# Gate sums on TensorE, one more MLP bank and a new head order in a gated attention and mixer kernel

## The chip, the cores and the metric

The kernel runs on one core of a Trainium2 chip. The metric is the time of one execution in microseconds (us), as the device gives it, and the median of the runs counts. The engines are named as the profile names them: PE is TensorE's matmul, PEld its weight load, DVE is VectorE, ACT is ScalarE, POOL is GpSimd, and SP is the queue that issues the DMAs.

## What is computed

The reference works on 4 batches of 768 tokens with 8 heads of 48 values, which makes 384 columns. Three layers follow each other.

```python
f = 1.0 / (1.0 + np.exp(-f_logit))
for t in range(S):                                  # gated linear attention, S = 768
    state = f[:, :, t, :, None] * state + einsum('bhd,bhe->bhde', k[:, :, t], v[:, :, t])
    y[:, :, t] = einsum('bhd,bhde->bhe', q[:, :, t], state)
xn = (x - mu) / np.sqrt(var + 1e-06) * g_ln         # x is y, heads side by side
x = x + np.maximum(xn @ w_ch1, 0.0) @ w_ch2         # first MLP, 384 -> 1536 -> 384
h = np.maximum(x.transpose(0, 2, 1) @ w_tok1, 0.0) @ w_tok2
u = x + h.transpose(0, 2, 1)                        # token mixing, 768 -> 256 -> 768
out = u + np.maximum(u @ w_ch1b, 0.0) @ w_ch2b      # second MLP
```

## The kernel before

The attention is cut into 24 units: unit n is chunk n // 4 (128 tokens) of batch n % 4. Within a unit the recurrence is turned into matrix products. The logarithms of the gates are summed along the 128 tokens, `ek` and `eq` are the exponentials of plus and minus these sums, K is multiplied by `ek` and Q by `eq`, and then masked products of K, Q and V and a carried state give `y`. The steps of a unit have short names, and the prediction uses them with the number of the unit in front, as in 3.y: `lf`, `lq`, `lv` load gates, K and Q, and V; `clamp` bounds the gate logits from below on DVE; `log` is an Exp and an Ln on ACT; `scan` is the running sum along the tokens on DVE (`tensor_tensor_scan`); `ek`, `eq` and `tot` are exponentials on ACT; `km` and `qm` are the two products; `kp` transposes K on PE and `kt` copies it out; `sc` and `st` are the score and state products on PE; `A0` and `A1` mask the scores on DVE; `stm`, `ste` and `std` carry the state on; `y` and `z` are the two halves of the output on PE, and `yw` is a one-element write between them, for which `z` waits; `lna`, `lnc` and `lnv` are the layer norm; `tp` transposes its result on PE, and `ah` and `al` split that into a high and a low part for the MLP.

The first MLP takes three units at a time, so it has 8 steps; steps 0 and 1 run as a pair. `m0.5` is block 5 (of 12) of the first product of step 0: nine matmuls of 384 columns in a PSUM bank. `m0.h5` on ACT and `m0.l5` on DVE (line L556) read this bank and write the hidden values' high and low parts `hh` and `hl`. `m0.o10` is a piece of the second product. The weights come as 64-bit numbers: `w5.ld` loads a block, `w5.a`, `.b` and `.c` turn it into fp32 on DVE (L201, L206, L211), `w5.h` rounds the high part on ACT and `w5.l` gives the rest, on DVE or POOL. `s` jobs do the same for the later layers' weights and store them in DRAM.

Each engine works through its instructions in the order in which they are recorded. Up to slot 77 (the head and the pair of steps 0 and 1) that order is the hand-written table `ORDER`; behind it each step has a slot number of its own, and the numbers are sorted. A `+45` behind an entry of the table puts 45 filler matmuls on zeros in front of this step's PE work: `busy` writes 224 columns, and `outp`, for `y`, writes three times as many matmuls of 64 columns. `WARM0` puts 56 fillers at the very start of PE.

PSUM has 8 banks: three in the pool `mmp` (first MLP blocks, second-product sums and `tp`), one in `atp` (`kp` alone) and four for the scores (`sc`). A bank of `mmp` goes round in turn, so a block waits until the block three places before it has been read by both ACT and DVE.

Token mixing and the second MLP (the `rt`, `ht`, L883 and L936 groups) begin behind step 7. The range check at the end decides on a flag whether a slow general path must be run; it isn't run with these inputs.

Of the kernel before, what the change touches and what calls it, by code (L numbers as in the profile page):

```python
# [29 lines left out]
JT = DTOK // 128  # L30
EPS = 1e-6
# [20 lines left out]
    1.ek 0.lq w14.ld 0.qm 1.lq w14.a 4.lf 2.scan 1.eq 0.km w12.ld 0.kp+45 4.clamp 1.qm 1.tot 2.ek 0.sc 4.log w2.ld
    w14.b 1.km 4.scan 3.ek 0.lv 0.tot 2.eq 0.kt w2.a 3.eq w12.a w2.b w12.b w14.c 3.tot 2.lq w14.h w2.c 1.kp+29
    1.sc 0.st 0.A0 0.A1 2.km 1.lv 5.lf 0.y+11 0.stm 1.kt w12.c 1.st 2.qm 0.yw 0.z 3.lq 0.ste 1.A1 0.lna 2.lv w14.l
    w4.ld 1.A0 1.stm 2.kp 5.clamp 1.y+3 w3.ld 0.lnc 1.ste 2.sc+8 5.log w1.ld 1.yw 2.kt 0.tp 3.km 5.scan 2.st 1.z
    2.A0 2.A1 3.kp 2.y+3 w2.h w12.h 2.stm 1.lna w2.l 3.qm 4.lq w12.l 1.lnc 2.ste 2.yw w1.a w3.a w4.a 3.lv 4.lv
    5.eq 4.ek 4.eq w1.b w3.b 5.ek w4.b 4.km w3.c w1.c 2.tot 0.ah w4.c 3.kt 3.sc+11 4.qm 0.lnv 1.tp 2.z 5.tot 2.lna
    w1.h 3.st w4.h 1.ah 3.A1 3.A0 4.kp 6.lf 2.lnc w3.h 4.kt 3.y+24 w0.ld 2.tp 4.sc 2.ah 1.lnv 4.st 3.stm 1.al
    4.tot 3.yw w5.ld 3.z 0.al 2.al 6.clamp w17.ld 4.A0 w1.l 4.A1 2.lnv w13.ld w5.a w3.l w4.l 3.lna 5.lq w0.a 6.log
    w5.b w16.ld 6.lv 0.std w0.b 3.ste m0.1 w5.c w5.h w5.l w0.c 6.scan 4.y m0.2 m0.h1 4.yw 4.stm 5.qm w0.h m0.h2  # L60
    m0.l1 m0.3 w0.l w22.ld m0.l2 4.z 3.lnc m0.h3 m0.4 m0.l3 w17.a w13.a 4.lna 5.km 6.lq 5.lv m0.0 7.lf 5.kp m0.h4
    6.eq 6.ek m0.h0 w15.ld w13.b w17.b w13.c m0.5 m0.l4 4.ste 5.sc 5.kt w13.h 4.lnc m0.h5 5.st w17.c 6.km m0.l0
    5.A1 3.tp 6.kp 4.tp 5.A0 3.ah 3.lnv m0.l5 6.qm 5.y w13.l w15.a w16.a 1.std 7.lv 7.clamp 6.sc w15.b w7.ld
    m0.o10 6.kt 4.ah 6.st 3.al 4.al w17.h w15.c 6.tot m0.o20 m0.o00 5.yw w16.b w17.l w16.c 6.A0 w15.h 5.stm w16.h
    w16.l w9.ld 5.z w15.l 2.lnr m0.o11 5.lna 7.log 6.A1 5.lnc m0.o21 w7.a w10.ld m0.r11 7.scan 5.tp 5.ah w7.b 5.al
    6.y 2.std w6.ld 7.lq 8.lf w7.c m0.r21 m0.o01 5.ste 6.yw m0.r01 7.tot 7.ek 7.eq m1.2 m1.0 w11.ld 6.stm w9.a
    m1.1 w10.a 4.lnv 7.km w10.b 8.clamp m1.h0 w9.b w7.h w9.c 6.z m1.h2 w18.ld m1.h1 8.lq m1.l0 m1.l2 w9.h w10.c
    m1.3 w9.l w6.a 7.kp w7.l m1.4 w22.a w6.b 8.log 7.qm m1.h3 m1.l1 m1.h4 w22.b m1.l3 7.sc w6.c w22.c w10.h w8.ld
    6.lna m1.5 w22.h 7.kt w22.l m1.h5 8.scan m1.l5 w11.a s1.ld m1.l4 w11.b 8.eq 6.lnc m1.o10 w6.h 7.st 4.std 10.lf
    m1.o20 8.tot 8.ek 5.lnv w11.c w10.l w8.a 5.lnr 9.lf w20.ld 6.ste 7.A0 7.A1 m1.o11 w11.h m1.o21 9.clamp 5.std  # L70
    9.log w8.b m1.o00 m1.r11 7.y m0.7 m1.r21 w8.c 3.std m1.o01 m0.h7 w6.l w20.a 9.scan m0.l7 7.yw 7.stm 8.km
    m1.r01 6.std w11.l m1.10 m1.9 m0.6 w8.h m1.h9 m0.h6 9.eq w19.ld w8.l 7.z 10.clamp m1.l9 8.qm 9.tot 10.log
    w18.a w19.a m1.7 w18.b 9.lq m0.l6 m1.h7 m1.h10 w20.b m1.l7 8.sc m1.l10 m1.8 w18.c m0.10 m1.h8 m0.8 m0.h10
    w18.h 9.ek w21.ld w20.c m1.l8 10.scan w19.b w18.l 9.km m0.h8 7.ste 8.kp w23.ld 9.lv m0.l8 8.lv w20.h 7.lna
    m1.6 11.lf 8.kt m0.9 10.lv 9.qm m1.h6 10.tot 8.st m0.h9 w20.l w19.c s0.ld m1.l6 w23.a w21.a 9.kp 10.eq 7.std
    9.kt m0.11 w23.b w19.h m0.h11 m0.l9 m0.l10 8.A0 6.tp 8.A1 w21.b m1.11 m0.l11 8.y m1.h11 w19.l 10.ek 6.ah 7.lnc
    w23.c 8.stm 8.yw w21.c m1.o12 8.z 9.sc s1.a w21.h 6.al w23.h s1.b w21.l m0.o22 m1.l11 8.ste 7.tp 11.clamp
    11.log w23.l 10.lq s0.a 9.st 7.lnv 8.lna m0.o23 9.A1 11.scan 11.ek 11.eq 9.stm 9.A0 m0.r23 9.ste m1.o13 9.y
    8.lnc m1.r13 6.lnv 10.km 7.ah 9.yw s1.c 10.qm m0.o02 8.tp 8.ah 8.al 10.kp 8.lnv 10.sc 7.al 9.z m0.o12 m0.o03
    10.kt 10.st s0.b m0.o13 10.stm m1.o02 10.A0 m0.r13 m0.r03 m1.o22 m1.d1 s3.ld m1.o03 9.std 9.lna 8.std 10.ste  # L80
    s0.c 10.A1 10.std s2.ld m0.d0 s0.h m0.d2 m1.o23 9.lnc m1.r03 11.lq 11.lv m1.d0 8.lnr m0.d1
""".split()

# [211 lines left out]

# [1045 lines left out]
```

## Time and profile before

| What | us |
|---|---|
| median of 3 runs (779.31 to 783.74) | 781.45 |
| the profiled execution | 782.92 |
| span of its trace, first to last instruction | 781.2 |
| PE busy in the span | 756.5 |

The span is what the trace shows, and the execution's own time is 1.7 us more. The execution that was profiled is 1.5 us above the median. The page gives busy time by engine and the chain that ended last; a window gives the busy time of each engine in one stretch; PEclk is the clock that TensorE was granted, where 1.00 is 2.4 GHz and 0.50 is 1.2 GHz.

### The profile page before, as it was taken

How to read it: one execution, taken by the hardware profiler on the slowest of the kernel's cores; microseconds unless marked ns; L12 is line 12 of the kernel's file. 1: busy time of each engine (PE TensorE's matmuls, PEld its weight loads, DVE VectorE, ACT ScalarE, POOL GpSimd, SP SyncE). 2: the span in 40 equal slices, each digit the busy share in tenths (PEclk: the TensorE clock that was granted, in tenths of full speed). 3: DMA queues.
4: the chain of work that ended last, by engine and by line, in shares of the span. 5: the costliest groups of instructions: out<-in, count | busy, mean ns of one | idle time of the engine just before them, and what ended most of it. 6: DMA issues, size and time to landing. Idle time of an engine off the chain costs nothing.

```text
span 781.2 us, 17469 instructions
## 1 busy us (share of the span) xinstructions
PE 756.5 (97%) x7129; PEld 735.0 (94%) x7129; DVE 516.9 (66%) x950; ACT 355.2 (45%) x851; POOL 152.9 (20%) x125
## 2 busy tenths in 40 slices
PE   8899999999999999999999999999999999999996
PEld 7689999989899898999999999999999999999996
DVE  7588877577787657765343664786558673878481
ACT  6454545244544444443131442564337442666440
POOL 1243333234444223330000010100001010101010
PEclk9999999999999999999999999999999999999999
DMA  8565442457647465553255985335343544343401
GB/s 249 152 217 178 149 142 77 150 166 230 216 147 230 137 183 189 168 186 123 74 161 212 344 305 177 93 113 160 110 143 102 161 126 134 99 144 101 137 21 66
DMA packets 61433, 122.54 MB, mean 157 GB/s; under 512 B 6944, under 2 KB 26784, under 8 KB 60576
## 3 DMA queue, kind: packets, MB, share of 16 engines
q1 hardware_dynamic: 61344, 121.33, 48.8%
q8 instruction: 58, 0.95, 0.5%
q14 instruction: 31, 0.25, 0.1%
HBM read 96.93 MB, written 24.38 MB: 155 GB/s over the span
## 4 chain that ended last, share of the span: by engine, by line
PE 86%; DVE 4%; DMA 3%; issue 2%; ACT 2%; POOL 1%; SPq 1%; POOLq 0%; DVEq 0%
PE mo L936 19%; PE mo L567 18%; PE mm L883 16%; PE mm L537 15%; PE rt L803 3%; PE ht L825 3%; PE sc L394 2%; PE sc L403 2%; DMA ts<-t_d 1%; PE sc L340 1%; PE sc L352 1%; PE tp L501 1%; PE kp L317 1%; PE tp L837 1%; DMA F<-in_f_t 1%
## 5 line engine op out<-in xcount | busy, mean ns | idle before, releaser
L537 PE MATMUL mm<-wx 128*128 128x384 f32 x864 | 161.5, 339 | 4.9 <-DVE hl L556 4.9
L537 PEld LDWEIGHTS mm<-wx 128*128 128x128 f32 x864 | 148.6, 188 | 8.0 <-DVE hl L556 7.5
L883 PE MATMUL mm<-xsh,wx 128*128 128x384 f32 x528 | 138.1, 335 | 0.9 <-DVE q L899 0.9
L567 PE MATMUL mo<-w2h,hh 128*128 128x384 f32 x288 | 99.0, 344 | 1.0 <-DVE hl L556 0.8
L883 PEld LDWEIGHTS mm<-xsh,wx 128*128 128x128 f32 x528 | 95.8, 188 | 1.5 <-PE mm L883 1.2
L936 PE MATMUL mo<-w2h,hh 128*128 128x384 f32 x288 | 97.0, 337 | 0.0
L567 PE MATMUL mo<-w2h,hl 128*128 128x384 f32 x288 | 96.4, 335 | 0.0
L567 PE MATMUL mo<-w2l,hh 128*128 128x384 f32 x288 | 96.3, 334 | 0.0
L936 PE MATMUL mo<-w2h,hl 128*128 128x384 f32 x288 | 96.3, 334 | 0.0
L936 PE MATMUL mo<-w2l,hh 128*128 128x384 f32 x288 | 96.2, 334 | 0.0
L923 POOL TENSOR_TENSOR hl<-u,hh 128x768 fp32r<-128x768 f32 x16 | 29.7, 1853 | 339.9 <-ACT u L918 246.0
L883 PE MATMUL mm<-xsl,wx 128*128 128x384 f32 x264 | 88.2, 334 | 0.0
L552 ACT ACTIVATE hh<-mm 128x384 fp32r<-128x384 f32 x96 | 46.3, 486 | 64.8 <-PE mm L537 60.1
L556 DVE SCALAR_TENSOR_TENSOR hl<-mm,hh 128x384 fp32r<-128x384 f32 x96 | 52.7, 551 | 27.5 <-ACT hh L552 27.2
L940 DVE TENSOR_TENSOR xr<-mo,xr 128x384 f32<-128x384 f32 x48 | 26.7, 556 | 54.2 <-PE mo L936 54.2
L1094 ACT ACTIVATE cs<-cs 128x384 f32<-128x384 f32 x56 | 31.1, 555 | 59.3 <-DVE cs L1091 59.1
L567 PEld LDWEIGHTS mo<-w2h,hh 128*128 128x128 f32 x288 | 54.1, 188 | 2.0 <-DVE hl L556 1.1
L936 PEld LDWEIGHTS mo<-w2h,hh 128*128 128x128 f32 x288 | 54.1, 188 | 0.1
L567 PEld LDWEIGHTS mo<-w2l,hh 128*128 128x128 f32 x288 | 54.1, 188 | 0.0
L936 PEld LDWEIGHTS mo<-w2l,hh 128*128 128x128 f32 x288 | 54.1, 188 | 0.0
L567 PEld LDWEIGHTS mo<-w2h,hl 128*128 128x128 f32 x288 | 54.1, 188 | 0.0
L936 PEld LDWEIGHTS mo<-w2h,hl 128*128 128x128 f32 x288 | 54.1, 188 | 0.0
(163 smaller groups left out, 1359.5 us busy)
## 6 DMA issues: line engine op xcount, KB each, us to landing
cs<-in_w SPq DMA_DIRECT2D x48, 384.0 KB, 3.1
sg<-in_w SPq DMA_DIRECT2D x44, 384.0 KB, 4.4
ts<-t_d SPq DMA_DIRECT2D x48, 256.0 KB, 3.0
wx<-f_d SPq DMA_DIRECT2D x6, 1152.0 KB, 11.4
V<-in_v_n SPq DMA_DIRECT2D x21, 288.0 KB, 4.7
F<-in_f_t SPq DMA_DIRECT2D x21, 224.0 KB, 3.6
T<-in_k_t SPq DMA_DIRECT2D x21, 224.0 KB, 2.7
T<-in_q_t SPq DMA_DIRECT2D x21, 224.0 KB, 3.2
```

Of the source, the lines that this page charges most:

```text
L394: nc.tensor.matmul(t["sc"][half(i), r, D * p:D * p + D], t["Q"][rows(r), p, half(i)], s[rows(r), D * p:D * p + D], start=False, stop=p == ...
L537: nc.tensor.matmul(ps, w[:, f, k, :], x[:, k, :], start=(i == 0), stop=(i == 8))
L552: nc.scalar.activation(out=hid(f)[0], in_=t[f], func=AF.Relu)
L556: nc.vector.scalar_tensor_tensor(hl, t[f], 0.0, hh.bitcast(F32), op0=ALU.max, op1=ALU.subtract)
L567: nc.tensor.matmul(ps, x, w[:, f, :], start=(f == lo and i == 0), stop=(f == hi and i == 2))
L803: nc.tensor.matmul(t["r"][j], w, x, start=(s == 0 and i == 0), stop=(s == NCH - 1 and i == 2))
L825: nc.tensor.matmul(ps, w, x[:, j], start=(i == 0), stop=(i == 5))
L883: nc.tensor.matmul(ps, w, x, start=n == 0, stop=n == len(ops) - 1)
L923: le.tensor_tensor(l, whole(g, i), h.bitcast(F32), op=ALU.subtract)
L936: nc.tensor.matmul(ps, x, w[:, f], start=(g % 3 == 0 and m == 0 and n == 0), stop=(g % 3 == 2 and m == 1 and n == 2))
L940: nc.vector.tensor_tensor(us[b, u], t["o", u], us[b, u], op=ALU.add)
L1094: nc.scalar.activation(out=t["u"], in_=t["u"], func=AF.Abs, accum_out=wlow[:, i:i + 1])
```

## The change

Sums by PE. For units 0 to 7 (`NSC`) a copy of the gate logits with tokens on the partitions, `f_n`, is loaded in place of `f_t`. `cum` multiplies its logarithm with the triangle `tri` in four fp32 matmuls that write a PSUM bank, and `ek`, `eq` and `tot` read that bank. The `scan` stays for units 8 to 23. The logits are no longer clamped in any unit: the Exp of `log` accumulates its sum into `wsum` instead, which is tested at the end with the other sums.

Banks. `kp`, `tp`, first-product blocks, second-product sums and `cum` now ask `bank4` for a bank. Inside the table the set `AT` names the 14 of them that take the bank of `atp`; behind it every fourth request takes it.

Hand-over. `yw` is a one-element copy on ACT and no longer a memset on DVE.

Copies. The set `OTHER` moves some `kt`, `w.h` to DVE and some `stm` copies to ACT. `POOL` has another list of products, and `VECTOR` takes five products of late units from POOL to DVE.

Order and slots. `ORDER` is a new table; its fillers are 13, 25, 7 and 3 where the old one had 45, 29, 11, 3, 8, 3, 11 and 24. `LATER` shifts `tp`, `kt`, `lq`, `log` and `lnc` of units 12 to 23 a little, `lnc` from 5 to 7.5 slots, and `JOBS` gives the later weights' jobs slots of their own. The fillers' zeros are a smaller tile that is read twice, with the same columns per matmul.

```diff
+PIECES = 56
+NSC = 8
 ORDER = """
-    0.lf 3.lf 0.clamp 0.log 1.lf 3.clamp 3.log 1.clamp 0.scan 2.lf 2.clamp 1.log 3.scan 1.scan 0.eq 0.ek 2.log
...
+    0.lf w4.ld 1.lf 3.lf 0.log 1.log 0.lq 0.cum 0.ek 0.eq w4.a 0.km 1.cum 0.lv w5.ld 0.kp+13 2.lf 4.lf 0.qm 0.sc
...
+LATER = dict(tp=11.05, kt=-6.25, lq=-12.75, log=-12.25, lnc=7.5)
...
+AT = set("""
+    cum0 cum3 kp3 tp1 m0.5 m0.2 m1.1 o020 o100 m0.9 m0.6 m1.11 o001 o011
+""".split())
...
+    def copy(name, o, i, dve=False):
+        if (name in OTHER) != dve:
+            nc.vector.tensor_copy(o, i)
+        else:
+            nc.scalar.activation(out=o, in_=i, func=AF.Copy)
...
-        def pre_clamp():
-            f = t["F"]
-            eng("clamp").tensor_scalar(f, f, -43.0, None, op0=ALU.max)
-
         def pre_log():
-            f = t["F"]
-            nc.scalar.activation(out=f, in_=f, func=AF.Exp, scale=-1.0)
+            f = t["L"]
+            nc.scalar.activation(out=f, in_=f, func=AF.Exp, scale=-1.0, accum_out=wsum[:f.shape[0], PIECES + n:PIECES + n + 1])
             nc.scalar.activation(out=f, in_=f, func=AF.Ln, bias=1.0)
...
+        def pre_cum(z=0):
+
+            ps = bank4(f"cum{n}", "cum")
+            busy(ps, z)
+            t["F"] = ps[:P2].rearrange("p (a c) -> p a c", a=NP)
+            for p in range(NP):
+                nc.tensor.matmul(t["F"][:, p], t["L"][:, P2 * p:P2 * p + P2], tri)
...
-            t["kp"] = atp.tile([128, 512], F32, tag="at", name="kp")
+            t["kp"] = bank4(f"kp{n}", "kp")
...
-            nc.vector.memset(done, 0.0)
+            nc.scalar.activation(out=done, in_=mhalf[:1, :1], func=AF.Copy)
...
+    def bank4(key, name):
+        turn["n"] += turn["on"]
+        at = turn["n"] % 4 == 3 if turn["on"] else key in AT
+        return (atp if at else mmp).tile([128, 512], F32, tag="at" if at else "mm", name=name)
...
     sl.run(P["J"], ORDER)
+    turn["on"] = True
+    sl.run(S7 - 1)
+    turn["on"] = False
     sl.run(S7 + 1)
```

Three places show what moved. The first is PE around the first MLP block: `sc<-zeros` are the fillers, `sc<-V,A` is a `y`, `tp<-` a transpose, `sc<-T` an `sc`, `sc<-mid` and `sc<-state` a `z`, and `mm<-wx` an MLP block. Before:

```order
L411 MATMUL sc<-zeros 128x64
L403 MATMUL sc<-V,A 64x48 x16
L501 MATMUL tp<-ident,first 128x128 x3
L340 MATMUL sc<-T 64x64 x16
...
L394 MATMUL sc<-mid,T 64x48 x8
L537 MATMUL mm<-wx 128x384 x9
L403 MATMUL sc<-V,A 64x48 x16
L537 MATMUL mm<-wx 128x384 x18
```

In the changed program, on the same engine at the same place:

```order
L441 MATMUL sc<-V,A 64x48 x16
L432 MATMUL sc<-mid,T 64x48 x8
L378 MATMUL sc<-T 64x64 x16
...
L332 MATMUL cum<-tri,F 112x128 x4
L582 MATMUL mm<-wx 128x384 x9
L441 MATMUL sc<-V,A 64x48 x16
L546 MATMUL tp<-ident,xn 128x128 x3
L332 MATMUL cum<-tri,F 112x128 x4
L432 MATMUL sc<-state_416,T 64x48 x8
```

In both programs the first block stands behind `kp`, `sc` and `st` of units 0 to 4, `y` and `z` of units 0 to 3 and `tp` of units 0 to 2. Now the sums of units 0 to 5 and 7 stand ahead of it too, the row of 72 fillers has gone, and behind the first block the work of units 3 to 5 comes before the second block.

The second place is DVE at the start of the program, behind its memsets: `first<-first` and `F<-F` at L284 are clamps, the L293 rows scans, L308 and L305 `qm` and `km`, and `cu` a weight conversion. Before:

```order
L284 TENSOR_SCALAR first<-first 112x512
L284 TENSOR_SCALAR F<-F 112x512
L284 TENSOR_SCALAR first<-first 112x512
L293 SCALAR_TENSOR_TENSOR first<-seg,first 112x512
L284 TENSOR_SCALAR first<-first 112x512
L293 SCALAR_TENSOR_TENSOR F<-seg,F 112x512
L293 SCALAR_TENSOR_TENSOR first<-seg,first 112x512
L308 TENSOR_TENSOR first<-first,eq 112x512
L201 TENSOR_SCALAR cu<-sg 128x384
```

Now, where L246 is a copy that `copy` puts on DVE:

```order
L223 TENSOR_SCALAR cu<-sg 128x384
L343 TENSOR_TENSOR first<-first,ek 112x512
L346 TENSOR_TENSOR first<-first,eq 112x512
L246 COPY kt<-kp 128x448
L228 SCALAR_TENSOR_TENSOR cu<-sg,cu 128x384
L233 SCALAR_TENSOR_TENSOR cu<-sg,cu 128x384
L223 TENSOR_SCALAR cu<-sg 128x384
L400 TENSOR_TENSOR A<-sc,upper 128x256
```

The four clamps and three scans that stood ahead of the first product have gone, and a copy of `kp` has come.

The third place is DVE in a late step, around the layer norm of one unit: `hl<-mm,hh` is the read of a block's bank, `xn<-sc,nm,gln` is `lnc` and `F<-seg,F` a scan. Before:

```order
L556 SCALAR_TENSOR_TENSOR hl<-mm,hh 128x384
L206 SCALAR_TENSOR_TENSOR cu<-sg,cu 128x384
L375 TENSOR_TENSOR mid<-sc,state_2282 112x192
L381 TENSOR_TENSOR state_3187<-sc,mid 112x192
L448 SCALAR_TENSOR_TENSOR xn<-sc,nm,gln 128x384
L293 SCALAR_TENSOR_TENSOR F<-seg,F 112x512
L556 SCALAR_TENSOR_TENSOR hl<-mm,hh 128x384
```

Now:

```order
L601 SCALAR_TENSOR_TENSOR hl<-mm,hh 128x384
L670 TENSOR_TENSOR sg<-cu,sg 128x384
L413 TENSOR_TENSOR mid<-sc,state_2158 112x192
L419 TENSOR_TENSOR state_3052<-sc,mid 112x192
L323 SCALAR_TENSOR_TENSOR F<-seg,F 112x512
L601 SCALAR_TENSOR_TENSOR hl<-mm,hh 128x384 x2
L223 TENSOR_SCALAR cu<-sg 128x384
L601 SCALAR_TENSOR_TENSOR hl<-mm,hh 128x384
L228 SCALAR_TENSOR_TENSOR cu<-sg,cu 128x384
L486 SCALAR_TENSOR_TENSOR xn<-sc,nm,gln 128x384
```

`lnc` has moved three reads of banks further back, so between two reads there is the scan but no longer both.

## Rows read from the trace of the kernel before

**Rows 1.** The page, part 1: busy us, share of the span, instructions.

```profile
PE 756.5 (97%) x7129; PEld 735.0 (94%) x7129; DVE 516.9 (66%) x950; ACT 355.2 (45%) x851; POOL 152.9 (20%) x125
```

**Rows 2.** Busy us of each engine in four stretches of the span, granted clock, DMA share.

```profile
0.00:47.50 47.50, 38.76 (x814) 34.35 (x814) 30.35 (x70) 25.68 (x59) 11.22 (x17) 0.93 0.68 203
47.50:372.00 324.50, 317.38 (x3993) 303.20 (x3992) 240.97 (x474) 150.57 (x371) 110.98 (x90) 1.00 0.53 168
372.00:775.10 403.10, 400.41 (x2327) 397.46 (x2325) 245.01 (x407) 178.95 (x423) 30.70 (x18) 1.00 0.45 144
775.10:781.20 6.10, 0.00 (x0) 0.00 (x0) 0.56 (x1) 0.00 (x0) 0.00 (x0) 0.77 0.13 42
```

**Rows 3.** Waits of PE: who for whom, us in total, times, longest.

```profile
PE mm L537 <- DVE hl L556: 4.9, 5, 1.4
...
PE kp L317 <- POOL T L305: 1.0, 1, 1.0
...
PE mo L567 <- DVE hl L556: 0.8, 1, 0.8
PE sc L394 <- DVE done L418: 0.7, 2, 0.5
```

**Rows 4.** Timeline of PE in the head: start, us, what.

```profile
1.10 8.37 PE L689 MATMUL warm<-zeros 128*128 128x224 bf16 x56 [1.10 <-DVE zeros L599]
9.31 4.48 PE L495 MATMUL kp<-zeros 128*128 128x224 bf16 x45
...
14.10 0.69 PE L340 MATMUL sc<-first 48*64 48x64 f32 x32
...
30.89 0.55 PE L501 MATMUL tp<-ident,first 128*128 128x128 f32 x3
...
47.48 1.83 PE L537 MATMUL mm<-wx 128*128 128x384 f32 x9
```

**Rows 5.** Chain that ended last, pieces in the head: start, us, what.

```profile
16.65 4.60 PE kp L495 x29
...
23.66 1.12 PE sc L411 x33
...
29.46 0.87 PE sc L495 x8
...
41.34 3.68 PE sc L411 x72
```

**Rows 6.** Timeline of ACT at the start: start, us, what.

```profile
8.21 0.61 ACT L298 ACTIVATE ek<-first 112x512 f32<-112x512 f32 x1
```

**Rows 7.** DVE by line and shape, 0 to 48 us: busy us, mean ns.

```profile
L293 DVE TENSOR_TENSOR_SCAN F<-seg,F 112x512 f32<-112x512 f32 x3 | 3.6, 1217 | 0.0
...
L284 DVE TENSOR_SCALAR F<-F 112x512 f32<-112x512 f32 x4 | 1.7, 423 | 0.5 <-DMA F<-in_f_t 0.5
L206 DVE SCALAR_TENSOR_TENSOR cu<-sg,cu 128x384 int32<-128x384 int32 x3 | 1.7, 551 | 0.0
...
L377 DVE COPY mid<-sc 112x192 f32<-112x192 f32 x4 | 1.4, 356 | 6.9 <-PE sc L403 6.9
```

**Rows 8.** PE by the microsecond in the head: busy us, granted clock, DMA share, GB/s.

```profile
15.00:16.00 1.00, 0.00 (x0) 1.00 1.05 260
...
18.00:19.00 1.00, 1.00 (x8) 0.50 0.70 171
34.00:35.00 1.00, 0.00 (x0) 1.00 0.00 0
...
40.00:41.00 1.00, 0.00 (x0) 1.00 0.89 332
```

**Rows 9.** Timeline of all engines around 210 us.

```profile
211.17 0.61 DVE L448 SCALAR_TENSOR_TENSOR xn<-sc,nm,gln 128x384 f32<-128x384 f32 x1
...
211.70 1.23 DVE L293 TENSOR_TENSOR_SCAN F<-seg,F 112x512 f32<-112x512 f32 x1
212.85 0.53 DVE L556 SCALAR_TENSOR_TENSOR hl<-mm,hh 128x384 fp32r<-128x384 f32 x1
```

More of the change, by code (lines that the diff above doesn't have):

```diff
@@ L52 @@
[L52 to L81, printed above, removed]
@@ new lines @@
+    w14.h 0.ah 1.lnc 3.kp 2.z 3.sc 1.std 3.kt 4.km 1.tp 4.lv 2.lna 2.ste 0.al 2.lnc w3.ld 3.st 4.kp 3.A0 4.qm
+    7.tot 4.tot 1.ah 7.eq 3.A1 2.tp 3.stm 6.lf 1.al w1.a 4.kt 2.ah 3.y+3 3.yw 3.z 4.sc 5.log w4.l w14.l w1.b 4.st
+    3.ste 3.lna 5.lq 2.al 5.cum w1.c 7.ek m0.5 4.A1 5.ek w1.h 6.log w1.l 4.A0 3.lnc 4.y 4.stm w3.a 3.tp 6.cum
+    w2.ld w0.ld 5.km 5.eq 4.yw 5.qm 4.z 3.ah 5.tot 3.al 1.lnv 5.lv w3.b w15.ld 6.ek w2.a 5.kp w0.a w3.c w2.b w0.b
+    5.sc m0.1 6.lq 4.lna 5.kt 5.st w3.h 4.ste 2.lnv 6.tot 5.stm 5.A0 m0.4 6.eq 5.A1 w3.l 5.y 0.lnv w2.c w0.c w2.h
@@ new lines @@
+    w2.l m0.h5 5.yw 5.ste m0.3 5.z 4.lnc m0.h1 m0.h4 9.lf 8.lf w12.ld m0.l5 m0.h3 m0.l1 m0.2 3.lnv 6.qm m0.l4 6.lv
+    w0.h 6.km 4.tp 5.lna 6.kp 6.sc w17.ld w16.ld m0.l3 5.lnc m0.h2 6.kt w0.l 4.ah 5.tp 7.lq 5.ah m0.0 6.st w15.a
+    2.std w12.a 7.km 8.log w15.b 4.al 5.al w15.c m1.0 m0.h0 m1.h0 8.scan 7.lv m0.l0 m0.l2 w15.h m1.4 6.A1 6.stm
+    w12.b 7.kp 7.kt w12.c w12.h 8.eq m1.1 7.qm 7.sc w16.a w15.l 6.A0 m1.l0 w12.l m1.h4 w13.ld m1.5 m1.l4 w17.a
+    w13.a w17.b 7.st w13.b w17.c 6.y m1.3 m1.2 8.lv w10.ld 6.ste w13.c w17.h 6.yw w13.h 8.tot m1.h5 m1.h1 w7.ld
@@ new lines @@
+    w16.b w17.l 8.ek w11.ld m1.l5 7.A1 7.A0 w16.c m1.l1 w7.a m1.h3 w13.l 6.z 4.std m1.h2 w8.ld w16.h 3.std 8.lq
+    m0.o10 w10.a w7.b w16.l m0.o20 9.log m1.l3 w7.c 8.qm 7.y m0.o00 m0.o11 9.scan m1.l2 w8.a w6.ld w7.h 7.stm
+    m0.o01 7.ste 2.lnr w10.b m1.o10 m0.o21 w7.l 8.km 5.lnv 7.yw w8.b w6.a 4.lnv m0.r11 w6.b m1.o11 w10.c w10.h
+    w8.c w9.ld 7.z 9.ek 6.lna 10.lf m0.r01 m1.o20 10.log 8.kp m0.r21 w20.ld 9.lq w6.c m1.o21 w6.h w10.l w11.a 9.eq
+    m1.o00 5.lnr m1.r11 9.tot w18.ld w6.l 6.lnc w11.b w8.h w9.a 11.lf w11.c w9.b w11.h w11.l m0.10 m1.r21 m1.o01
@@ new lines @@
+    8.sc 8.kt 10.scan w8.l w18.a m0.h10 s1.ld w19.ld 6.tp w20.a w20.b w20.c w18.b w9.c 8.st w9.h m0.l10 w9.l
+    m1.r01 w18.c 6.lnv m1.10 m1.7 8.stm 10.lv m1.h10 m1.h7 m0.9 w23.ld 5.std w19.a m1.l10 m1.l7 s0.ld m0.h9 w20.h
+    w19.b m0.7 m0.h7 10.tot m0.8 9.qm m0.l9 7.lna w19.c w21.ld m0.h8 10.ek m0.6 m0.l7 w22.ld w19.h 8.A0 w18.h
+    w19.l m0.h6 8.A1 8.y m0.l8 m1.9 9.km m0.l6 7.lnc m1.h9 11.log w20.l 9.sc w21.a m1.l9 w22.a w18.l 8.yw 9.lv
+    9.kp m1.11 10.eq 8.ste m1.h11 m0.11 w22.b w23.a 8.z 9.kt w23.b 9.st 6.std m0.h11 w22.c m1.l11 w23.c 9.A0 7.tp
@@ L85 @@
+""".split())
 class Slots:
@@ L253, in eng @@
         def eng(x):
-            return nc.gpsimd if n >= P["NV"] or f"{n}.{x}" in POOL else nc.vector
+            return nc.gpsimd if n >= P["NV"] and f"{n}.{x}" not in VECTOR or f"{n}.{x}" in POOL else nc.vector
         def load_f():
-            t["F"] = first[:P2, 12 * n + 8:12 * n + 12, :] if n < 3 else sb.tile([P2, NP, C], F32, tag="F", name="F")
-            nc.sync.dma_start(out=t["F"], in_=f_t[n])
+            f = first[:, 12 * n + 8:12 * n + 12, :] if n < 3 else sb.tile([128, NP, C], F32, tag="F", name="F")
+            if n < NSC:
+                t["L"] = f.rearrange("p a c -> p (a c)")[:, :NP * P2]
+                nc.sync.dma_start(out=t["L"], in_=f_n[n])
+            else:
+                t["L"] = t["F"] = f[:P2]
+                nc.sync.dma_start(out=f[:P2], in_=f_t[n])
         def load_q():
@@ L321, in ktrans_e @@
             t["kt"] = s1.tile([128, NP * P2], F32, tag="kt", name="kt")
-            nc.scalar.activation(out=t["kt"], in_=t["kp"][:, :NP * P2], func=AF.Copy)
+            copy(f"{n}.kt", t["kt"], t["kp"][:, :NP * P2])
         def rows(r):
@@ L376, in stat_m @@
             else:
-                nc.vector.tensor_copy(t["S"][1], new(0))
+                copy(f"{n}.stm", t["S"][1], new(0), True)
         def stat_e():
@@ L410, in outp @@
             for _ in range(3 * z):
-                nc.tensor.matmul(t["sc"][:, 0, 448:], zeros[:, :128], zeros[:, :64])
+                nc.tensor.matmul(t["sc"][:, 0, 448:], zeros[:, 0], zeros[:, 0, :64])
             inner()
@@ L459, in trans @@
         def trans(z=0):
-            t["tp"] = transposes(t["xn"], z)
+            t["tp"] = transposes(n, t["xn"], z)
         last = c == NCH - 1
@@ L470, in attention @@
         for d, add, f, name in (
-                (-13, sl.e, pre_clamp, "clamp"), (-12, sl.e, pre_log, "log"), (-11, sl.e, pre_sum, "scan"),
+                (-12, sl.e, pre_log, "log"), (-11, sl.e if n >= NSC else sl.p, pre_sum if n >= NSC else pre_cum, "scan" if n >= NSC else "cum"),
                 (-10, sl.e, pre_ek, "ek"), (-10, sl.e, pre_eq, "eq"), (-7.5, sl.e, pre_qm, "qm"),
@@ L484, in attention @@
             if f:
-                add(s0 + d, f, f"{n}.{name}")
+                add(s0 + (LATER.get(name, d) if n > 11 else d), f, f"{n}.{name}")
     def follow(i, j):
```

66 lines of the change are left out of this document (45 added, 21 removed).

## The prediction, made before the changed kernel ran

> **What bounds the kernel now.** I read the page's busy times first: PE is busy in 97% of the span, DVE in 66%, ACT in 45% and POOL in 20% [rows 1]. So time is won only where PE does something useless or waits. Then I cut the span at the first MLP block, at the change to the later layers and at the last matmul [rows 2]. In the first 47.5 us PE is busy for 38.8, but the timeline shows that much of this is filler: 56 matmuls on zeros in 8.37 us, 45 more in 4.48, and the first block starts only at 47.48 [rows 4]. From 47.5 to 372.0 PE lacks 324.5 - 317.4 = 7.1 us, from there to 775.1 it lacks 2.7, and the last 6.1 us are the stores' end. The list of PE's waits [rows 3] says what the 7.1 are: 4.9 us in five waits of a block for DVE's `hl`, 1.0 for a `km` on POOL, 0.8 for a second product's `hl`. The chain that ended last shows what delays the first block: fillers lie on it with 4.60, 1.12, 0.87 and 3.68 us [rows 5], because a filler before a `y` writes the bank that the masks read and so can't start early.
>
> So two things can give time: an earlier first block, up to some 10 us, and up to 5 us of waits for banks. What stands behind the first block is some 720 us of PE work that the change leaves as it is.
>
> **The first block, 47.48 now.** The same 26 pieces of attention stand ahead of it as before; the terms are these.
>
> Fillers out: 4.60 + 1.12 + 0.87 + 3.68 = 10.3 us of the chain [rows 5].
>
> Fillers left: a wide one takes 4.48 / 45 = 0.10 us [rows 4], a narrow one 1.12 / 33 = 0.034 [rows 5]. 13 wide ones cost 1.3, and the 7 and 3 are 21 and 9 narrow ones, 0.7 and 0.3. The 25 in front of 2.cum (2.5 us) are covered by the wait for ScalarE: unit 2's logarithm stands behind that of unit 3, a state copy and an `eq`. I count 2.3, and 4.8 if that cover is gone.
>
> A sum on PE has no row. From below, three transposes of 128 columns take 0.55, so four of them 0.73; from above, an `sc` puts 16 matmuls of 64 columns through in 0.69 with four at a time on different quarters of the array, which is 2.76 one at a time, and half as many columns then take 1.4 [rows 4]. I take 1.0, the middle. The Trainium skill (FP8 and Floating Point Precision, TensorE Precision Notes) says that true fp32 goes through the array in four passes; for 512 columns at 2.4 GHz that is an estimate of 0.85, by which the final sum would be 0.7 us lower. No run here shows it yet.
>
> First unit: 0.cum is queued behind the 56 start fillers, which end at 1.10 + 8.37 = 9.47 [rows 4]; with its own 1.0 the first `ek` can start at 10.5. It started at 8.21 [rows 6]. That costs 2.3.
>
> Five more sums (units 2, 3, 4, 7, 5) stand on PE ahead of the first block; 1.cum lies beside unit 0's exponentials. PE still waits for others in the head, so I lay half on the path, 2.5; bounds 0 and 7.0, five at 1.4.
>
> DVE: six scans of 1.22 and seven clamps of 0.42 leave its first 48 us, 10.3 us of 30.4 [rows 2, 7]. Against that come three copies of `kp` (a copy of 192 columns takes 0.36, so 448 take under 0.83) and a weight's high part; but two weights fewer are converted by then, at 0.55 for each of two steps and some 0.35 for the first [rows 7], which about cancels. DVE idles for PE in between, so the relief doesn't all arrive: I take a third, 3.4, with bounds 0 and 10.3.
>
> Sum: -10.3 + 2.3 + 2.3 + 2.5 - 3.4 = -6.6, and the first block starts at about 41. Bounds: with no relief from DVE, all five sums at 1.4 and all fillers on the path the saving is gone (-10.3 + 4.8 + 2.3 + 7.0 = +3.8); with the full relief and hidden sums it is -16. Neither end is likely, since DVE works 30 of 47 us there; I use -11 and -1.
>
> **Behind it.** 6.cum falls where PE is full: +1.0. After its first block PE now meets `y`, `tp`, a sum, `z`, `kp` and `sc` before the second, where it used to get two blocks and more. Each of them needs DVE or ACT just before. I add 1.0 of new idle time, bounds 0 and 3.
>
> Banks: around 211 us DVE does `lnc` (0.61) and a scan (1.23) between two `hl` [rows 9], and the block three places further waits. The change parts `lnc` from the scan by three `hl` and gives a fourth bank, worth about one block, 1.83 us [rows 4]; the longest wait is 1.4 [rows 3]. But `kp` now takes banks from the same round. I take 4.5 of the 4.9, with bounds 5.9 (the `km` wait too) and -2 (new waits of `kp`).
>
> At nothing: `yw` on ACT. Its two waits were 0.7 in total [rows 3]; in late units `tp`, `sc` and `st`, some 1.8 us on PE, lie between `y` and `z` and hide it. Without that cover it costs up to one ACT instruction, 0.6 [rows 6], a unit. What queues behind `yw` on ACT is the next `hh`; ACT is under half busy. The accumulated sum in `log` adds a short read on ACT, hidden likewise. Clamps of late units come off POOL, which waits anyway. The later layers keep their order.
>
> **Sum.** -6.6 + 1.0 + 1.0 - 4.5 = -9.1. From the profiled execution, 782.92, that gives 773.8; the median of the runs was 1.5 below it, so 772.3.
>
> **Rivals.**
>
> *The clock falls (slower).* Twice PE stood still for nearly 2 us and then ran at 0.50: after 15 to 16 us and after 40 to 41 [rows 8]. The fillers that go are what made PE busy there. If the head runs at 1.2 GHz, its 26 small pieces of about 0.6 [rows 4] and seven sums take twice as long, 23 us more. The time of before is reached where 9.1 of these lie on the path, and 0.5% above it at 13; with two thirds on the path it would be about 788. Against it: PE also stood still in 34 to 35 and kept 1.00 [rows 8], and the removed waits are themselves the gaps. The Trainium skill (TensorE: Matmul & The Clock Gate, What's actually happening) says that the throttled clock is the default and activity releases it, which speaks for this rival; the trace agrees in that both drops followed a gap. I give it 8%.
>
> *The head isn't bound by fillers.* The DMA share is 0.68 over the first 47.5 us and above 1 at 15 to 16 [rows 2, 8]; if loads, or ACT, which now does sums, copies and `yw`, set the chain, the first block comes at 46 and only -1.5 is left of -6.6: -4.0, 777.4. For it: 0.cum is late, and unit 0 leads the rest. Against: DMA falls to 0.00 at 34 to 35 while PE still waits for DVE. 17%.
>
> *The banks give nothing.* `hl` is late by DVE's order, the scans of late units stay, and `kp` shares. Then -6.6 + 2.0 = -4.6: 776.9. Against it stands the third place of the order, where `lnc` has moved. 15%.
>
> **How the numbers follow.** The forecast has 60%, its own range 766 to 776; the three rivals 8, 17 and 15. A difference under 0.5%, 3.9 us, is what a measurement can't tell from none; faster is below 777.5. The two rivals in the middle end at 777, on either side of that line, so 0.60 and a good half of 0.32 are faster: 0.79. The rest of them and the mild part of the first give 0.15 for the same, and 0.06 is left for slower. The range takes in -11 in the head with 4.9 from the banks and 1 of costs, -15 in all and 766.4, a little below that for a cheaper `cum`, and above the middle rivals, 779.5.
>
> **What would show it.** PE's first block (L582) at 39 to 43 us instead of 47.5; fillers in the head 3 to 6 us besides the start's; a `cum` of four matmuls in 0.8 to 1.4 us; PE's waits for `hl` under 1 us in total; no new wait of `sc<-state` or `sc<-mid` for `done` above 1 us; at most one or two drops to 0.50 in the head. The prediction is wrong if the first block starts above 45, if PE idles for more than 4 us in the 20 us behind it, or if `kp` or blocks wait for banks as long as before.

## The result, and the profile after

The changed kernel takes 771.85 us (median of 4 runs, 767.28 to 772.87). The kernel before took 781.05 beside it. The ratio is 0.9868, with a 95% interval from 0.9819 to 0.9917. The forecast was 772.3. The profiled execution took 772.87 us, with a span of 771.2.

First the busy times of the changed kernel, cut at its first MLP block, at 372 us and at the last matmul. The columns are those of [rows 2].

```profile
0.00:43.90 43.90, 38.00 (x721) 33.77 (x722) 23.27 (x51) 23.85 (x67) 8.77 (x15) 0.88 0.60 183
43.90:372.00 328.10, 327.87 (x4051) 314.15 (x4050) 238.48 (x475) 153.49 (x404) 84.79 (x73) 1.00 0.55 174
372.00:765.60 393.60, 391.75 (x2278) 389.36 (x2276) 241.33 (x399) 177.67 (x419) 30.67 (x18) 1.00 0.46 145
765.60:771.20 5.60, 0.01 (x1) 0.00 (x0) 0.56 (x1) 0.00 (x0) 0.00 (x0) 0.96 0.13 45
```

The span is 10.0 us shorter, and against [rows 2, 4] it divides so. The first block comes 3.6 us earlier (43.90 instead of 47.48). Behind it up to 372 us PE lacks 328.10 - 327.87 = 0.23 us where it lacked 7.1. From there to the last matmul it lacks 1.85 instead of 2.7, and the end is 0.5 shorter. PE's work behind the first block grew by 1.8 us, 1.04 of it the sum of unit 6 (its row stands below); what the rest is was not traced. So -3.6 - 6.9 - 0.8 - 0.5 + 1.8 = -10.0.

The waits of PE in the changed kernel, as in [rows 3]: who for whom, total, times, longest.

```profile
PE sc L441 <- issue: 3.2, 1, 3.2
PE warm L735 <- DVE zeros L644: 1.1, 1, 1.1
...
PE cum L332 <- ACT first L319: 0.5, 1, 0.5
...
PE mm L582 <- DVE hl L601: 0.2, 1, 0.2
```

Of 4.9 us of waits for `hl` 0.2 are left, and the waits of `kp` for POOL and of `mo` for `hl` are gone. At the top stands something that no step of the prediction had: 3.2 us in which PE waited for nothing that the profile shows.

The head of PE, to be held against [rows 4]: start, duration, what, and in brackets the idle time ahead of it.

```profile
1.05 8.04 PE L735 MATMUL warm<-zeros 128*128 128x224 bf16 x56 [1.05 <-DVE zeros L644]
8.93 1.91 PE L332 MATMUL cum<-tri,first 128*112 128x128 f32 x16
10.68 1.41 PE L540 MATMUL kp<-zeros 128*128 128x224 bf16 x13
...
13.79 2.57 PE L540 MATMUL cum<-zeros 128*128 128x224 bf16 x25
16.86 1.13 PE L332 MATMUL cum<-tri,first 128*112 128x128 f32 x8 [0.50 <-ACT first L319]
...
31.31 0.34 PE L441 MATMUL sc<-firstv,A 64*64 64x48 f32 x2 [3.20 <-issue]
...
43.90 1.82 PE L582 MATMUL mm<-wx 128*128 128x384 f32 x9
46.65 1.04 PE L332 MATMUL cum<-tri,F 128*112 128x128 f32 x8
```

Two sums take 1.91 us together, so about 0.95 each. The 25 fillers are covered: behind them PE still waits 0.50 for ScalarE's logarithm. The stop falls into the `y` of unit 2, between 28.11 and 31.31.

PE by the microsecond around that stop, with the columns of [rows 8]:

```profile
27.00:28.00 1.00, 1.00 (x37) 1.00 1.03 393
28.00:29.00 1.00, 0.11 (x8) 1.00 1.11 399
29.00:30.00 1.00, 0.00 (x0) 1.00 0.91 346
30.00:31.00 1.00, 0.00 (x0) 0.56 0.16 53
31.00:32.00 1.00, 0.69 (x17) 0.50 0.04 15
...
40.00:41.00 1.00, 0.97 (x40) 0.82 0.09 25
```

PE stands still while the DMA engines are full, the granted clock falls to 0.50 at 30.1, and it stays there until 40.3, for 10.2 us. In the DMA view of 28 to 29 us a fetch of instructions stands among the loads (packets, MB, share of 16 engines):

```profile
q8 instruction: 1, 0.02, 6.9%
```

### The profile page after: what moved, and what is told of

It reads as the page before. It is cut to its first block, busy times and chain, and to the rows that moved or that the text cites. A ratio compares the mean times of both kernels' runs of the same rounds, so it can differ in the third digit from the quotient of the medians.

```text
span 771.2 us, 17321 instructions
## 1 busy us (share of the span) xinstructions
PE 757.6 (98%) x7045; PEld 737.3 (96%) x7045; DVE 503.6 (65%) x924; ACT 355.0 (46%) x889; POOL 124.2 (16%) x106
## 4 chain that ended last, share of the span: by engine, by line
PE 94%; DVE 2%; ACT 1%; DMA 1%; issue 1%; SPq 0%; ACTq 0%
PE mo L985 19%; PE mm L582 19%; PE mo L612 18%; PE mm L932 17%; PE rt L852 3%; PE ht L874 3%; PE sc L432 2%; PE sc L441 2%; PE sc L378 2%; PE tp L546 1%; PE sc L390 1%; PE kp L355 1%; PE cum L332 1%; DMA ts<-t_d 1%; PE warm L735 1%; PE tp L886 1%
## 5 line engine op out<-in xcount | busy, mean ns | idle before, releaser
L582 PE MATMUL mm<-wx 128*128 128x384 f32 x864 | 159.7, 338 | 0.2 <-DVE hl L601 0.2
```

The source lines that it names most:

```text
L582: nc.tensor.matmul(ps, w[:, f, k, :], x[:, k, :], start=(i == 0), stop=(i == 8))
```

## The experiments

Times are medians; the kernel before, run beside them on the same chips, had medians of 781.7 to 783.3. What counts more than a microsecond's difference of medians is the profile of each.

**Behind the first block: banks, `lnc`, or the logarithm.** One part alone in the kernel before:

```diff
-            t["kp"] = atp.tile([128, 512], F32, tag="at", name="kp")
+            t["kp"] = bank4("kp", "kp")
...
+        turn["n"] += turn["on"]
+        at = turn["n"] % 4 == 3 if turn["on"] else key == "kp"
...
+    turn["on"] = True
+    sl.run(S7 - 1)
+    turn["on"] = False
```

> The kernel before with one part alone: from 77 on blocks, products and keys' transposes take the four banks in turn; nothing else is changed. My theory: of the 7.1 us that TensorE lacks between 47.5 and 372 us, the five waits for hl and the one of a product go (5.7 us), the one for a key on GpSimd (1.0) stays: time 3 to 6 us under before, 775 to 779. Rival, banks are nothing without the new order: within 1.5 us of before.

It took 782.66 us, ratio 1.0002 [0.9977, 1.0026]. The waits of its PE between 60 and 372 us:

```profile
PE mm L544 <- DVE hl L563: 5.1, 5, 1.6
PE kp L317 <- POOL T L305: 1.0, 1, 1.0
```

They are nearly as before [rows 3]; they only fall two blocks later, and from 47.5 to 372 us PE lacks 6.8 us instead of 7.1. My theory failed; why the lateness outlasts one more bank was not traced. The reverse, the changed kernel with the old banks in the later stages:

```diff
-        at = turn["n"] % 4 == 3 if turn["on"] else key in AT
+        at = key.startswith("kp") if turn["on"] else key in AT
```

> The changed kernel, but from 77 on (behind the written order) the keys' transposes have the fourth bank for themselves again and all blocks and products share three, as before; the other places of the later stages stay new. My theory: the fourth bank is worth most of the 5 us of waits for hl that the kernel before had there: 2 to 5 us of them come back, time 774 to 777 beside some 771.5 for the changed kernel. Rival, the order did it, since lnc and the scan no longer stand together: under 1 us of waits, time 771 to 772.5.

It took 772.90 us (771.68 to 773.41). Its PE has no wait at all above 0.2 us between 60 and 372 us; from 47.5 to 372 it lacks half a microsecond, all of it a wait for a load at 50.9:

```profile
47.50:372.00 324.50, 323.99 (x3965) 310.05 (x3966) 236.62 (x467) 149.54 (x392) 86.36 (x72) 1.00 0.54 172
```

So the fourth bank alone brings nothing that can be seen, and by this test the rival, `lnc`, would have it. Its own test:

```diff
-LATER = dict(tp=11.05, kt=-6.25, lq=-12.75, log=-12.25, lnc=7.5)
+LATER = dict(tp=11.05, kt=-6.25, lq=-12.75, log=-12.25)
```

> The changed kernel with lnc of the later units at its old place (5 instead of 7.5), next to the scan; four banks stay. My theory: four banks take up a lateness of one block, so at most 1 us of waits for hl comes back: 771 to 773. Rival, the order did it: 2 to 5 us of waits, 774 to 777.

It took 771.75 us, and the waits for `hl` stay at:

```profile
PE mm L582 <- DVE hl L601: 0.5, 2, 0.2
```

Neither did it alone; both put back together were not run. I then looked at who is late ahead of the scan in the kernel before. ScalarE at 207 us, behind the transposes:

```profile
207.49 0.49 ACT L519 ACTIVATE wx<-tp 128x384 fp32r<-128x384 f32 x1 [3.29 <-PE tp L501]
207.88 0.62 ACT L288 ACTIVATE F<-F 112x512 f32<-112x512 f32 x1
208.53 0.63 ACT L289 ACTIVATE F<-F 112x512 f32<-112x512 f32 x1
209.07 0.47 ACT L552 ACTIVATE hh<-mm 128x384 fp32r<-128x384 f32 x1
```

ScalarE idles 3.29 us for the transposes and only then does the next unit's logarithm (the two `F`), with a block's `hh` queued behind it. VectorE needs that `hh`, and its row says how long it stood:

```profile
209.57 0.56 DVE L556 SCALAR_TENSOR_TENSOR hl<-mm,hh 128x384 fp32r<-128x384 f32 x1 [1.00 <-ACT hh L552]
```

Everything behind it on VectorE, `lnc` and the scan of [rows 9] among it, is 1.0 us late, and PE's wait of 1.29 at 213 us follows. The same microsecond of idling precedes the waits at 164, 264 and 313 us. The changed kernel places the logarithm at -12.25 instead of -12, a quarter of a step that puts it into that idle time. One number in the kernel before:

```diff
-                add(s0 + d, f, f"{n}.{name}")
+                add(s0 + (-12.25 if n > 11 and name == "log" else d), f, f"{n}.{name}")
```

> The kernel before with one number changed: the logarithms of units 12 and later stand at -12.25 instead of -12, which puts their two ScalarE instructions ahead of the high part of the transposes instead of ahead of a block's hh. Neither the banks nor the place of lnc explained the vanished waits; in the trace of before, VectorE idles for 1.00 us for hh at 159.29, 208.57, 258.65 and 308.76 us, with 1.2 us of logarithm ahead of that hh on ScalarE, and in the changed kernel this idling is gone. My theory now: this alone removes the waits for hl, 4.9 us to under 1.5; the 1.0 us for a key on GpSimd stays; TensorE lacks under 3.5 us between 60 and 372 us instead of 7.1, time 2.5 to 5 us under before. Rival: it takes the loads' new due times or the other moved places too: waits for hl stay above 3.5 us, time within 1.5 us of before.

It took 776.34 us, ratio 0.9924 [0.9896, 0.9952]: 5.4 us less. Its ScalarE and VectorE at the same place:

```profile
205.22 0.49 ACT L519 ACTIVATE wx<-tp 128x384 fp32r<-128x384 f32 x1 [1.78 <-PE tp L501]
205.61 0.49 ACT L552 ACTIVATE hh<-mm 128x384 fp32r<-128x384 f32 x1
```

```profile
205.75 0.56 DVE L523 TENSOR_TENSOR wx<-tp,wx 128x384 fp32r<-128x384 f32 x1 [1.02 <-ACT wx L519]
206.22 0.55 DVE L556 SCALAR_TENSOR_TENSOR hl<-mm,hh 128x384 fp32r<-128x384 f32 x1
```

`hh` follows the transposes at once, and `hl` follows without idling. The waits between 60 and 372 us are now:

```profile
PE mm L537 <- DVE hl L556: 1.0, 3, 0.5
PE mo L567 <- DVE hl L556: 0.8, 1, 0.8
```

From 47.5 to 372 us PE lacks 324.50 - 322.35 = 2.15 us instead of 7.1:

```profile
47.50:372.00 324.50, 322.35 (x4024) 308.67 (x4024) 240.24 (x477) 151.32 (x369) 109.64 (x90) 1.00 0.54 170
```

The first block of this profile came at 46.14 instead of 47.48, because the clock did not fall in front of it; the stretch from 47.5 on leaves that out.

The wait of `kp` for POOL went too, which I hadn't expected; the key's factor is an exponential of the scanned logarithm, which now comes earlier. So 5.0 of the 6.9 us behind the first block come from one number in the kernel before. What takes the remaining 1.9 (`lnc`, the banks, the other shifted slots, products moved off POOL) was not separated, and the changed kernel with its logarithm back at -12 was not run.

**The hand-over.**

```diff
-            nc.scalar.activation(out=done, in_=mhalf[:1, :1], func=AF.Copy)
+            nc.vector.memset(done, 0.0)
```

> The changed kernel with the hand-over done by a memset on VectorE again instead of ScalarE. I costed the move at nothing. My theory: waits for done of at most 0.7 us in all more or less, time 770.5 to 773. Rival, the hand-over queued behind VectorE's work is worth much in the head or in late units: waits for done of 2 us or more, time 774 or more.

It took 771.70 us, with 0.2 us of waits for `done`: nothing, as costed.

**The head: fillers and sums.** The kernel before without its fillers (the start's 56 stay):

```diff
-0.kp+45
+0.kp
...
-3.y+24
+3.y
```

(and so for `1.kp+29`, `0.y+11`, `1.y+3`, `2.sc+8`, `2.y+3` and `3.sc+11`)

> The kernel before with every filler in the order removed (45, 29, 11, 3, 8, 3, 11, 24); the 56 at the start stay. By my theory 10.3 us of filler lay on the chain ahead of the first block, but the chain falls back on VectorE once they are gone, so about half arrives: first block at 41 to 44 instead of 47.48, time 776 to 779 (-2 to -5). Rival, the clock: the pieces of the head run at 1.2 GHz for over 10 us, the first block stays at 46 or later and the time at 781 or more. Rival, the head isn't bound by fillers: first block at 46 to 48, time within 2 us of before. If all 10.3 us arrive: first block at 37 to 38, time 771 to 772.

It took 778.55 us, ratio 0.9952 [0.9926, 0.9978], with its first block at 43.40. Its head, and its largest wait there:

```profile
0.00:43.40 43.40, 31.45 (x598) 26.84 (x598) 31.21 (x72) 26.06 (x60) 11.66 (x17) 0.62 0.75 221
```

```profile
PE kp L317 <- DVE first L305: 4.7, 1, 4.7
```

The mean clock of 0.62 is the rival's half clock, from 11 to 45 us without a break, and yet the first block comes 4.1 us earlier. Fillers did hold the clock at 2.4 GHz for most of the head, but what they sped up was worth less than their own length, since PE waited for VectorE anyway. The Trainium skill (TensorE: Matmul & The Clock Gate, What's actually happening) says that the throttled clock is the default and activity releases it; the 0.62 of this row beside 0.93 with the fillers [rows 2] agrees.

The changed kernel without its fillers (13, 25, 7 and 3), of which the largest is:

```diff
-2.cum+25
+2.cum
```

> The changed kernel without its four fillers (13, 25, 7, 3). My theory: the 25 are covered by a wait for ScalarE, the others (1.41 and 0.77 and 0.53 us) are on the chain in part: first block 0.5 to 2 us earlier than 43.90, time 770 to 772. Rival, fillers hold the clock: more than the 10 us at 0.50 that the changed kernel shows, first block 1 us or more later, time 774 or more.

It took 769.73 us (768.72 to 770.82), first block at 41.73. Where the 25 stood, PE now waits for the same logarithm:

```profile
PE cum L332 <- ACT first L319: 3.0, 1, 3.0
```

That is 2.57 + 0.50 almost to the tenth: the cover held. The half clock lasted 10.2 us in all, as in the changed kernel, in other places (from 14.5 and from 35 us). PE stopped for 1.02 us at 26.5. A second profile of the changed kernel (below), with a stop of 1.00, had its first block at 41.11, so the fillers left cost nothing that the first block shows.

The changed kernel with fillers back where the kernel before had them:

```diff
-3.sc
+3.sc+11
...
-3.y+3
+3.y+24
```

> The changed kernel with 11 fillers back ahead of 3.sc and 24 (72 narrow ones instead of 9) ahead of 3.y, as the kernel before had them. My theory: some 1.1 and 2.1 us of filler, more at half clock, on the chain: first block 2 to 5 us later, time 774 to 777. Rival, they hold the clock up and pay for themselves: less than 10 us at 0.50, time 772 or less.

It took 770.64 us, first block at 42.38. My expectation of 774 to 777 was wrong: the profile I compared with had a long stop, this one a stop of 0.72 and 3.4 us at half clock. Beside the 41.11 of the second profile the fillers cost 1.3 us, and the median is no longer for them.

The changed kernel with scans instead of sums:

```diff
-            if n < NSC:
+            if n < SUMS:
...
-2.cum+25
+2.scan
```

(`SUMS` is 0, and each `cum` of the order is a `scan` at the same place.)

> The changed kernel with the running sums of all units as scans on VectorE again (and so without the 25 fillers that stood ahead of the third sum); the clamps stay away, and the order is that of the changed kernel. My theory: eight scans of 1.22 us come onto VectorE and some 8 us of sums leave TensorE; VectorE leads in the head, so the first block comes 1 to 4 us later than 43.90, time 773 to 776. Rival, the sums bring all of the head's gain: first block at 47 or later, time 776 to 780. Rival, the sums bring nothing, fillers all: first block at 43.5 or earlier, time 772 or less.

It took 775.78 us (774.14 to 778.94). Its first block came early, at 41.98, but that misleads; the second shows the delay:

```profile
41.98 1.86 PE L583 MATMUL mm<-wx 128*128 128x384 f32 x9
...
47.99 0.77 PE L433 MATMUL sc<-state,T 48*64 48x48 f32 x10 [2.15 <-ACT done L457]
...
51.49 2.71 PE L583 MATMUL mm<-wx 128*128 128x384 f32 x9
```

In the changed kernel the second block starts at 49.65, and VectorE works 27.5 us up to there. Here it works 34.6 us up to 51.5 us, and PE's mean clock is 0.75:

```profile
0.00:51.50 51.50, 37.72 (x753) 32.82 (x753) 34.58 (x68) 30.76 (x82) 9.47 (x16) 0.75 0.64 190
```

The waits of PE up to 60 us are above all for the hand-over, the masks and `mid`:

```profile
PE sc L433 <- ACT done L457: 5.0, 3, 2.5
PE sc L442 <- DVE A L401: 3.6, 2, 2.8
PE sc L450 <- ACT mid L249: 2.4, 1, 2.4
```

So sums (with the 25 fillers that went with them) are worth 4 us. Some of that may be the clock's: it stood at 0.50 for 27 us of the first 54 here and for 10.2 in the changed kernel, and the two were not separated. The clamps stayed away in this run, so it says nothing of them.

**The stop.** The changed kernel once more, unchanged:

> The changed kernel as it is, once more. In its profile TensorE stood still for 3.20 us at 28.11 us, waiting for nothing that the profile shows, with an instruction fetch that began to move only at 28.7 us, among loads at a DMA share above 1; the kernel with more fillers is the same up to there, had its fetch at 25.9 and stood for 0.72. My theory: the stop is chance, set by how long the fetch stands behind the loads: this run's fetch lies somewhere between 25 and 29 us, the stop between 0.5 and 3.5, single times spread from 767 to 773, and a profile with a short stop has its first block at 41 or earlier. Rival, the stop belongs to the program: 3 us at the same place, first block at 43.5 to 44.3, times within 1 us of 772.

It took 771.16 us. Its stop was a third of the first one's, and its first block came at the time forecast:

```profile
29.90 0.26 PE L441 MATMUL sc<-firstv,A 64*64 64x48 f32 x2 [1.00 <-issue]
...
41.11 1.83 PE L582 MATMUL mm<-wx 128*128 128x384 f32 x9
```

So the stop's length differs between runs of one and the same kernel. Two orders of the loads, the first with three of them taken from their old places to the load of unit 6's gates:

```diff
-3.stm 6.lf 1.al
+3.stm 6.lf w1.ld 4.lv w3.ld 1.al
```

> The changed kernel with three loads (parts w1 and w3, and unit 4's v, 1.06 MB in all) behind the sixth unit's gates, so issued at about 34 us instead of 23 to 25, when DMA is idle; their readers come after 39 us. My theory: the loads in the queues delay TensorE's fetch; with half of them gone from 25 to 29 us the stop falls under 1 us, the 10 us at half clock behind it shrink or go, the first block comes at 38 to 41 and the time is 766 to 769. Rival, the stop has nothing to do with these loads: a stop of 1 to 3 us stays, first block at 42 to 44, time 770 to 772. Other rival, the late loads are missed: VectorE waits for w1 or TensorE for unit 4, time 773 or more.

The second has this besides, and again the old places are empty:

```diff
-0.lna 7.lf 1.kt
+0.lna 3.lq 4.lq 3.lv 7.lf 1.kt
```

> As the run with later loads, and besides the loads of units 3 and 4 (k, q and unit 3's v) ahead of the load of the seventh unit's gates, which waits for a buffer: they are issued at about 13 us instead of 20 to 23, so DMA works through from 13 to 20 us. My theory: nearly no loads are left at 25 to 29 us, no stop above 0.5 us there; but fetches at 15 to 20 us now stand among loads, so a stop can come there instead: first block at 38 to 41, time 765 to 769. Rival, no link between loads and stop: 770 to 772.

The first took 769.43 us; its stop of 1.55 and half clock of 3.4 us missed what I expected (under 1). The second took 767.98 (766.89 to 768.40), ratio 0.9808 [0.9770, 0.9846]: 3.2 us under the changed kernel's 771.16 beside it, and below seven of the changed kernel's eight runs. Its PE and, from the DMA side, the microseconds of its fetch and its stop:

```profile
28.99 0.26 PE L441 MATMUL sc<-firstv,A 64*64 64x48 f32 x2 [0.33 <-issue]
...
38.64 1.66 PE L582 MATMUL mm<-wx 128*128 128x384 f32 x8
```

```profile
26.00:27.00 1.00, 0.90 (x30) 1.00 0.07 16
...
28.00:29.00 1.00, 0.67 (x28) 1.00 0.00 0
```

The clock stays at 1.00 from 10 to 50 us. All eight profiles with this stop in the same `y`, the fetch's start read in windows of a tenth; "ready" is the end of the stop less its length:

| kernel | ready | fetch starts | PE goes on | fetch to going on | stop | half clock, during or behind | first block |
|---|---|---|---|---|---|---|---|
| changed | 28.11 | 28.7 | 31.31 | 2.6 | 3.20 | 10.2 | 43.90 |
| the same again | 28.90 | 27.2 | 29.90 | 2.7 | 1.00 | 3.4 | 41.11 |
| loads later | 28.09 | 27.1 | 29.64 | 2.5 | 1.55 | 3.4 | 40.80 |
| loads spread | 28.66 | 26.3 | 28.99 | 2.7 | 0.33 | none | 38.64 |
| more fillers | 27.60 | 25.9 | 28.32 | 2.4 | 0.72 | 3.4 | 42.38 |
| three banks | 27.15 | 29.2 | 31.64 | 2.4 | 4.49 | 6.8 | 42.81 |
| `lnc` at its old place | 27.59 | 28.4 | 30.87 | 2.5 | 3.28 | 3.4 | 42.11 |
| hand-over on VectorE | 29.21 | 29.7 | 32.13 | 2.4 | 2.92 | 6.8 | 43.29 |

PE goes on 2.4 to 2.7 us after the fetch starts, however late that is. That ties the stop to the fetch. That loads delay the fetch rests on less. PE starts the 7 fillers of this `y` at 26.01 to 28.03 in the eight profiles; against that moment the fetch came 1.2 us early with empty queues (loads spread, fillers at 27.51), and between 0.5 early and 3.2 late (three banks, 26.01) where loads stood in them. But only one profile has empty queues.

## Why the prediction was right, and where it was not

The time was right (771.85 beside 772.3), in part by luck: two of its terms reached their size by other ways than I gave, and misses cancel. In the profiled execution the first block came 3.0 us later than forecast (43.90, not 40.9), and PE's work behind it grew by 0.8 more (1.8, not 1.0). Against that its idle time up to 372 us fell by 6.9, where the forecast had 4.5 - 1.0 = 3.5, and 1.3 behind it (0.8 and 0.5) had no term. 3.0 + 0.8 - 3.4 - 1.3 = -0.9 is the way from -9.1 to -10.0.

**Fillers out, -10.3.** Over-sized. In the kernel before, alone, 4.1 us arrive at the first block (778.55 in all): PE then waits 4.7 us for a key on VectorE, and it works at 0.50. **Fillers left, +2.3**: their length is 1.41 + 0.77 + 0.53 = 2.7, and the 25 are covered, as argued. That the 2.7 lie on the path is not shown: without them the first block came at 41.73, with them at 41.11, after stops of 1.02 and 1.00.

**First unit, +2.3**: its first `ek` starts at 10.00, not 8.21 [rows 6], +1.8:

```profile
10.00 0.60 ACT L336 ACTIVATE ek<-cum 112x512 f32<-112x512 f32 x1 [3.38 <-PE cum L332]
```

The kernel before did `eq` ahead of that `ek`, the changed one does it behind; the pair ends at 11.08 instead of 8.82, +2.3. **A sum at 1.0**: 0.95 for each of the first two, 1.04 to 1.13 for one alone. The estimate of 0.85 from the four passes of the Trainium skill (FP8 and Floating Point Precision, TensorE Precision Notes) is somewhat low here.

**DVE's relief (-3.4) less five more sums (+2.5).** Taken together nearly nothing, -0.9; putting the scans back costs 4 us, some of it perhaps by the clock. So what arrived of the relief I under-sized, and what the fillers gave I over-sized. The two errors nearly cancel in the first block: 41.11 in the second profile of the changed kernel, where the forecast said 41. That this is so close is luck, for 41.11 has a stop of 1.00 and 3.4 us at half clock in it.

**The first block at 39 to 43** failed in the first profile, 43.90. No term had the stop of 3.2 us and the 10.2 us at half clock that came with it. The trace of the kernel before could have told of it: there PE stood for 0.80 us from 27.47, waiting for nothing that the profile shows, and no term took that up:

```profile
28.27 0.32 PE L317 MATMUL kp<-ident,first 112*128 112x112 f32 x1 [0.80 <-issue]
```

**6.cum, +1.0**: 1.04. **New idle time, +1.0**: it didn't come; PE lacks 0.23 us from the first block to 372 us.

**Banks, -4.5.** The size was near by luck (5.0 from one number, 6.9 in all), the mechanism wrong. The step that failed is "the change parts `lnc` from the scan by three `hl` and gives a fourth bank": four banks alone bring 0, taking them away costs no wait, and `lnc` back costs 0.3 us of waits. What I missed stands one engine ahead. I read which VectorE work lay before the late `hl` and didn't ask why VectorE had stood idle just before it. The logarithm on ScalarE had held up an `hh`, and a quarter step of it brings the 5.0. The rival "the banks give nothing" was thus right about the banks and wrong about the time.

**The clock falls.** In the changed kernel it did for 10.2 us, and in the kernel before without fillers for 34, but its price of up to 23 us was too high: in that kernel the first block came 4.1 us earlier all the same. **The head isn't bound by fillers** was half true: fillers alone give 4.1 us in the kernel before, and the change in all 6.4 in its second profile (47.48 to 41.11).

**`yw` on ACT at nothing**: 771.70 beside 771.85. Right.

One reading in the chances is off: the two rivals in the middle, 777.4 and 776.9, both end below the line at 777.5, not on either side of it.

## What to carry to other kernels

When an engine that feeds the bound one does its work late, follow the chain to the first engine that idles, here ScalarE, before blaming the long instructions in between; a quarter step of one due time gave 5 us where a bank gave none. A filler is worth what the chain gives back once it is gone, not its own length. One profile of a head with full DMA queues is a sample: take two before a difference of 3 us is explained.

## What the runs showed of the hardware

In eight profiles PE stopped for 0.3 to 4.5 us at one place, waiting for nothing that the profile shows. The page of the profile counts 57 instruction packets of 0.93 MB on one queue, some 16 KB each, and PE went on 2.4 to 2.7 us after such a packet began to move. In the run without fillers, where the stop lay in another `y`, it was 3.6, with a packet that took 2.2 us itself instead of 1.0 to 1.3. The Trainium skill (Runtime: NRT & Kernel Launch, Instruction fetch mechanics) says that a sequencer fetches its next 16 KiB of instructions by its own DMA queue while it executes the current ones, and that the cost is mostly hidden. Here, among many short matmuls and in all but one profile with loads in the queues, 0.3 to 4.5 us of it were not.

Of eight profiles of the changed kernel and its variants with a stop of 0.7 us or more, seven show the granted clock at 0.50, which is 1.2 GHz, for 3 to 10 us during the stop or just behind it; in the one without fillers it stayed at 1.00 for 7 us more.
